# Linear attention in front of a gated layer: chunks of 128 steps worked as two halves, with a new order written out in the source

## The chip, the core and the metric

The kernel runs on one core of a Trainium2 chip. Its time is the device time of one execution in microseconds (us). The kernel before takes 587.41 us (median of 3 runs, 586.96 to 587.76). A change is called no change where it lies within 0.2%, about 1.2 us.

The core has a matrix engine (TensorE, PE in the profile; its weight loads are listed apart as PEld), VectorE (DVE), ScalarE (ACT) and GpSimd (POOL). Each runs its own list of instructions in order and waits for the others by semaphores. SyncE (SP) issues nearly all transfers.

## The reference

Four batches, 8 heads, 768 steps, 48 numbers a head. A state of 48x48 per batch and head decays by `w` at each step and takes in `k v`; the outputs of all heads, 384 numbers a token, go through a gated layer of width 1536.

```python
for t in range(S):
    cur = np.einsum('bhd,bhe->bhde', u[None] * kt, vt)
    y[:, :, t] = np.einsum('bhd,bhde->bhe', rt, state + cur)
    state = wt[:, :, :, None] * state + np.einsum('bhd,bhe->bhde', kt, vt)
...
g = x @ w_gate;  silu = g * (1.0 / (1.0 + np.exp(-g)));  val = x @ w_val
return silu * val @ w_out
```

## The kernel before

**Attention.** The 768 steps of a batch are cut into 6 chunks of 128 steps, 24 chunks in all (`n`, one batch after the other). Two heads share the 112 partitions of a tile (rows 0 to 47 and 64 to 111), so there are four pairs `p`, each with heads `j` = 0 and 1. For a chunk, `scan` and `scan2` (VectorE) make running products of `w`, `kq` and `re` scale `k` and `r` by them. On TensorE, `kb` transposes the scaled `k` (tile `kb`, copied out by `kn` on ScalarE), `sc` multiplies `k` and `r` into 128x128 scores per head, `dl` makes the chunk's addition to the state, and `y` sums the output from the scores (`at`, with `vt` and `vz`) and from the state before the chunk (`kr` with `sp`). `diag` puts the `u` term on the diagonal of `at` with eight ScalarE products of 128x128; `pred` (VectorE, twice, one for each `j`) copies the scores above the diagonal over it. `sps`, `spb` and `st` carry the state (VectorE, ScalarE, VectorE). `xh` and `xl` split the output into two parts; for the first ten chunks `xm` on TensorE makes the difference for `xl`. In `sc`, `dl` and `y` the operands are fp32, and the trace shows each such product as two passes (two MATMUL records).

**Gated layer.** The tokens form groups of 4, 2, 4, 4, 4, 4, 2 chunks. For each of 12 slices `f` of the width, `gv` runs 9 products for the gate (j=0) and 9 for the value (j=1) over all tokens of the group, `silu`, `sg`, `hh`, `hl` turn them into two parts, and `po` adds them to the group's output with 3 products a chunk. `ob` and `out` store it.

**Weights.** They arrive as 64-bit words (`raw`) and are turned into two parts by `top`, `low`, `upper` (ScalarE) and `shift`, `sign`, `plus`, `lower` (VectorE), for each `f` once. The first group's `gv` of slice `f` waits for it.

**Order.** A table `ORDER` holds the first part of the work, to the end of group 2; each name in it issues one step on its engine. From group 3 on a loop (`attention_steps` and `behind`) spreads the attention, three pieces to a chunk, between blocks of the gated layer. `spin` issues idle products at the start, which keep TensorE's clock up while it has nothing to do. In PSUM the attention has a pool `psA` with two buffers of one bank, `gv` two banks and `po` four.

Of the kernel before, what the change touches and what calls it, by code (L numbers as in the profile page):

```python
# [39 lines left out]
FREE = 3  # L40
# [3 lines left out]
TAKEN = 10  # L44

AGAIN = 10
# [1 line left out]
spin:21 uh ws:0 kr:0 ws:1 kr:1 raw:0 vt:0 scan:0 vt:1 kr:2 ub:0 seed:0 whole:0 raw:1 prod:0 kq:0
kr:3 scan2:0 kb:0 spin:6 re:0 kn:0 ws:2 diag:0:0 prod:1 sc:0 spin:19 scan:1 diag:0:1 pred:0:0
whole:1 seed:1 kq:1 top:0 pred:0:1 scan2:1 dl:0 spin:7 low:0 st:0 ws:3 shift:0 kb:1 vz:1 vz:0 re:1  # L50
y:0 sign:0 kn:1 diag:1:0 sc:1 spin:11 vt:2 prod:2 kr:4 diag:1:1 plus:0 xh:0 pred:1:0 raw:2 upper:0
xm:0 spin:9 pred:1:1 xl:0 sps:1 lower:0 top:1 dl:1 spin:10 spb:1 st:1 shift:1 low:1 y:1 spin:5
scan:2 sign:1 whole:2 xh:1 vt:3 vz:2 kr:5 xm:1 spin:7 sps:2 xl:1 kq:2 spb:2 plus:1 kb:2 spin:5
seed:2 kn:2 raw:3 prod:3 upper:1 dl:2 spin:13 scan2:2 diag:2:1 st:2 ws:4 re:2 diag:2:0 lower:1
sc:2 spin:18 top:2 scan:3 low:2 pred:2:0 kq:3 vz:3 seed:3 whole:3 kb:3 pred:2:1 scan2:3 y:2 spin:4
kn:3 diag:3:0 shift:2 ws:5 re:3 vt:4 xh:2 sps:3 sc:3 diag:3:1 sign:2 xm:2 spin:8 spb:3 pred:3:0
xl:2 pred:3:1 top:3 dl:3 plus:2 y:3 spin:12 low:3 st:3 raw:4 scan:4 upper:2 vt:5 prod:4 xh:3
lower:2 vz:4 xm:3 spin:5 whole:4 xl:3 gv:0:0:0 kq:4 shift:3 seed:4 sign:3 gv:0:0:1 silu:0:0
scan2:4 top:4 plus:3 vz:5 ws:6 gv:0:1:0 low:4 re:4 raw:5 upper:3 sg:0:0 kb:4 scan:5 hh:0:0
gv:0:1:1 kn:4 lower:3 whole:5 diag:4:0 hl:0:0 diag:4:1 sc:4 seed:5 shift:4 po:0:0 sps:4 silu:0:1  # L60
sign:4 spb:4 top:5 sg:0:1 gv:0:2:0 plus:4 hh:0:1 low:5 hl:0:1 raw:6 pred:4:1 gv:0:2:1 upper:4
pred:4:0 silu:0:2 lower:4 po:0:1 sg:0:2 shift:5 hh:0:2 prod:5 dl:4 sign:5 gv:0:3:0 top:6 kq:5
low:6 st:4 gv:0:3:1 plus:5 hl:0:2 upper:5 raw:7 sps:5 kb:5 scan2:5 silu:0:3 po:0:2 nat:6 kn:5
diag:5:0 sg:0:3 ws:7 lower:5 hh:0:3 gv:0:4:0 hl:0:3 shift:6 re:5 po:0:3 silu:0:4 sign:6 top:7
scan:6 low:7 y:4 plus:6 whole:6 gv:0:4:1 diag:5:1 vt:6 seed:6 ru:6 raw:8 ruk:6 upper:6 a0:6 kr:6
gv:0:5:0 sg:0:4 nat:7 diag:6:0 lower:6 vz:6 hh:0:4 gv:0:5:1 shift:7 xh:4 spb:5 hl:0:4 sign:7
silu:0:5 po:0:4 top:8 sg:0:5 plus:7 hh:0:5 xm:4 gv:0:6:0 low:8 kq:6 raw:9 hl:0:5 upper:7 scan2:6
gv:0:6:1 silu:0:6 lower:7 ws:8 xl:4 re:6 sc:5 shift:8 po:0:5 sg:0:6 sign:8 hh:0:6 top:9 hl:0:6
gv:0:7:0 low:9 plus:8 scan:7 upper:8 raw:10 gv:0:7:1 pred:5:0 silu:0:7 whole:7 seed:7 lower:8
po:0:6 sg:0:7 shift:9 hh:0:7 gv:0:8:0 pred:5:1 sign:9 top:10 y:5 hl:0:7 low:10 plus:9 po:0:7  # L70
silu:0:8 kr:7 ru:7 upper:9 raw:11 ruk:7 a0:7 diag:6:1 lower:9 vt:7 kb:6 nat:8 gv:0:8:1 kn:6
shift:10 xh:5 diag:7:0 kq:7 xm:5 gv:0:9:0 sign:10 xl:5 sg:0:8 plus:10 hh:0:8 sc:6 top:11 gv:0:9:1
hl:0:8 pred:6:0 upper:10 pred:6:1 scan2:7 po:0:8 silu:0:9 low:11 lower:10 ws:9 vz:7 dl:6 ru:8 y:6
shift:11 gv:0:10:0 sg:0:9 diag:7:1 kr:8 vt:8 sign:11 hh:0:9 st:6 gv:0:10:1 plus:11 hl:0:9 upper:11
kb:7 re:7 po:0:9 silu:0:10 ruk:8 vz:8 lower:11 kn:7 a0:8 gv:0:11:0 sg:0:10 diag:8:0 nat:9 scan:8
hh:0:10 gv:0:11:1 sps:7 whole:8 kq:8 spb:7 seed:8 hl:0:10 scan2:8 silu:0:11 po:0:10 xh:6 ru:9
ws:10 re:8 ruk:9 xm:6 gv:1:0:0 sg:0:11 xl:6 a0:9 hh:0:11 gv:1:0:1 scan:9 nat:10 sc:7 hl:0:11
whole:9 seed:9 silu:1:0 po:0:11 pred:7:1 sg:1:0 pred:7:0 hh:1:0 ru:10 dl:7 ob:0:0 hl:1:0 gv:1:1:0
ob:0:1 ruk:10 out:0:0 out:0:1 st:7 y:7 sps:8 silu:1:1 po:1:0 diag:8:1 vt:9 kr:9 kb:8 gv:1:1:1
diag:9:0 a0:10 nat:11 gv:1:2:0 spb:8 sg:1:1 hh:1:1 gv:1:2:1 xh:7 hl:1:1 vz:9 silu:1:2 kn:8 po:1:1  # L80
sg:1:2 ob:0:2 kq:9 hh:1:2 out:0:2 xm:7 ob:0:3 gv:1:3:0 scan2:9 xl:7 out:0:3 sc:8 hl:1:2 ws:11 re:9
# [36 lines left out]
def recurrence_then_glu_kernel(  # L118
# [114 lines left out]

    def shift(f):
        ints[f] = wst.tile([P, 3, DM], U32, tag="s", name=f"s_{f}", bufs=1)
        t = raws[f][:, :, :, 1].bitcast(U32)
        keep(nc.vector.tensor_scalar(ints[f], t, 0x1FFFFFFF, 3, ALU.bitwise_and, ALU.logical_shift_left))

    def sign(f):
        t = raws[f][:, :, :, 1].bitcast(U32)  # L240
        keep(nc.vector.scalar_tensor_tensor(ints[f], t, 0x80000000, ints[f], ALU.bitwise_and, ALU.bitwise_or))
# [536 lines left out]
```

## Time and profile before

| | |
|---|---|
| median of 3 runs | 587.41 us |
| profiled execution, first to last instruction | 585.2 us |
| TensorE busy | 570.4 us, 97% |
| VectorE, ScalarE busy | 325.1 us, 283.9 us |
| first `gv` starts | 46.59 us |
| last `po` ends | about 577.7 us |

Busy time of TensorE counts idle products too, and a matmul's record includes the time that it takes to run through the array, so that records overlap. For what a step costs, the start of the next one is read, not the length of a record. A group row reads: line, engine, operation, written tile <- read tiles, rows*columns of the weights, moving operand, count | busy us, mean ns of one | idle time before it and what ended it. A timeline row begins with the start and the length in us.

### The profile page before, as it was taken

Reading aid. Unit: us, or ns where it says so; the run is one execution under the profiler, and the core shown is the slowest. Engines: PE = TensorE matmul, PEld = TensorE weight load, DVE = VectorE, ACT = ScalarE, POOL = GpSimd, SP = SyncE. Lnnn points to the kernel's source line nnn. Section 1 sums busy time; section 2 is a strip of 40 time slices with the busy share of each in tenths; the row PEclk is TensorE's granted clock in tenths of the full one; section 3 lists DMA queues with packets and bytes.
Section 4 is the critical chain, followed back from the end, with each engine's and each line's share of the span. In section 5 each row is a group of like instructions: output and inputs, shape, how many; then the busy total and the mean of one; then the engine's idle time right before and its main releaser. Section 6 shows DMA issues by size and latency. Waiting matters only on the chain.

```text
span 585.2 us, 12525 instructions
## 1 busy us (share of the span) xinstructions
PE 570.4 (97%) x5333; PEld 494.4 (84%) x5333; DVE 325.1 (56%) x511; ACT 283.9 (49%) x639; POOL 1.8 (0%) x11
## 2 busy tenths in 40 slices
PE   7999999999999999999999999999999999999994
PEld 5777888889999888788888888888888888889994
DVE  6999999995655349751456365446344332222221
ACT  5798766864546236551525334475556422122221
POOL 1000000000000000000000000000000000000000
...
GB/s 302 262 129 192 125 222 168 176 89 123 92 61 62 55 48 138 115 55 1 106 39 89 41 50 88 103 88 96 62 74 62 55 2 0 1 1 7 48 1 33
DMA packets 22334, 50.63 MB, mean 87 GB/s; under 512 B 2592, under 2 KB 8864, under 8 KB 22272
## 3 DMA queue, kind: packets, MB, share of 16 engines
...
q8 instruction: 44, 0.72, 0.5%
...
q10 hardware_dynamic: 16, 0.00, 0.0%
...
## 4 chain that ended last, share of the span: by engine, by line
PE 83%; ACT 6%; DMA 5%; DVE 4%; issue 1%; SPq 0%; ACTq 0%; DVEq 0%
PE gv L541 46%; PE po L575 24%; PE y L441 5%; PE sc L385 4%; DMA raw<-in_wo_dram 2%; PE idle L608 2%; ACT at L346 1%; PE kb L361 1%; PE dl L409 1%; ACT raw L227 1%; DVE et L306 1%; DMA kr<-in_kr_dram 1%; DMA u_two<-in_u_rows_dram 1%; ACT raw L232 1%; ACT w_h L248 1%
## 5 line engine op out<-in xcount | busy, mean ns | idle before, releaser
L541 PE MATMUL gv<-xh,w_h 128*128 128x512 f32 (+1 forms) x504 | 183.7, 365 | 0.0
L541 PE MATMUL gv<-xl,w_h 128*128 128x512 f32 (+1 forms) x504 | 182.0, 361 | 0.0
L541 PE MATMUL gv<-xh,w_l 128*128 128x512 f32 (+1 forms) x504 | 181.6, 360 | 0.0
L553 DVE TENSOR_TENSOR sg<-sg,gv 128x512 f32<-128x512 f32 (+1 forms) x84 | 51.1, 608 | 141.4 <-PE gv L541 138.3
L541 PEld LDWEIGHTS gv<-xh,w_h 128*128 128x128 f32 x504 | 94.7, 188 | 15.1 <-issue 1.8
L541 PEld LDWEIGHTS gv<-xl,w_h 128*128 128x128 f32 x504 | 94.7, 188 | 15.0
L541 PEld LDWEIGHTS gv<-xh,w_l 128*128 128x128 f32 x504 | 94.8, 188 | 12.9
L575 PE MATMUL po<-w_h,hh 128*128 128x384 f32 x288 | 100.8, 350 | 0.5 <-ACT hh L558 0.5
L575 PE MATMUL po<-w_h,hl 128*128 128x384 f32 x288 | 97.2, 337 | 0.3 <-DVE hl L563 0.3
L558 ACT ACTIVATE hh<-sg 128x512 fp32r<-128x512 f32 (+1 forms) x84 | 47.8, 569 | 101.2 <-DVE sg L553 89.4
L575 PE MATMUL po<-w_l,hh 128*128 128x384 f32 x288 | 96.8, 336 | 0.0
L550 ACT ACTIVATE sg<-gv 128x512 f32<-128x512 f32 (+1 forms) x84 | 44.6, 531 | 90.8 <-PE gv L541 81.5
L563 DVE TENSOR_TENSOR hl<-sg,hh 128x512 fp32r<-128x512 f32 (+1 forms) x84 | 51.5, 613 | 51.1 <-ACT hh L558 50.7
L575 PEld LDWEIGHTS po<-w_h,hh 128*128 128x128 f32 x288 | 54.0, 188 | 7.5 <-issue 4.6
L575 PEld LDWEIGHTS po<-w_h,hl 128*128 128x128 f32 x288 | 54.1, 188 | 2.2 <-DVE hl L563 1.1
L575 PEld LDWEIGHTS po<-w_l,hh 128*128 128x128 f32 x288 | 54.0, 188 | 0.0
L346 ACT ACTIVATE at<-ident,a 128x128 f32<-128x128 f32 x144 | 45.6, 390 | 5.6 <-PE y L441 4.2
L390 DVE COPY_PREDICATED at<-mask,sc 128x512 f32<-128x512 uint32 x48 | 33.3, 730 | 8.7 <-PE sc L385 8.6
L317 ACT ACTIVATE ws<-ws 112x517 f32<-112x517 f32 x24 | 15.3, 638 | 35.3 <-DVE et L306 22.0
L289 DVE TENSOR_TENSOR_SCAN qt<-ws,d1q 112x516 f32<-112x516 f32 x24 | 29.4, 1226 | 1.8 <-DMA ws<-in_wt_dram 1.7
L306 DVE TENSOR_TENSOR_SCAN et<-ws,d1e 112x516 f32<-112x516 f32 x24 | 29.4, 1225 | 1.5 <-ACT pend L294 1.4
L385 PE MATMUL sc<-kr 48*64 48x128 f32 x768 | 28.6, 282 | 1.3 <-ACT kn L371 0.5
...
## 6 DMA issues: line engine op xcount, KB each, us to landing
...
```

The costliest lines, as they stand in the source:

```text
L289: keep(nc.vector.tensor_tensor_scan(_flat(qts[n])[:, ::-1], wss[n][:, 1:][:, ::-1], _flat(d1q)[:, ::-1], 0.0, ALU.mult, ALU.add))
L306: keep(nc.vector.tensor_tensor_scan(_flat(ets[n]), wss[n][:, :L], _flat(d1e), 0.0, ALU.mult, ALU.add))
L346: keep(nc.scalar.activation(a[:, p, :], ident, AF.Copy, scale=d))
L385: pin(nc.tensor.matmul(scs[n][j][ms, p, :], krs[n][o, 0, p, ms], krs[n][o, 1, p, :], start=True, stop=True,))
L390: keep(nc.vector.copy_predicated(ats[n, j], mask4, scs[n][j]))
L441: pin(nc.tensor.matmul(ys[n][32 * q : 32 * q + 32, b // 4, :], lhs, rhs, start=start[q] == i, stop=stop[q] == i,))
L541: pin(nc.tensor.matmul(ps, a[:, f, j, q * P : (q + 1) * P], x[:, q, :], start=m == 0, stop=m == 3 * NK - 1,))
L550: keep(nc.scalar.activation(sgs[g, f], ps, AF.Silu))
L553: keep(nc.vector.tensor_tensor(sgs[g, f], sgs[g, f], gvs.pop((g, f, 1)), ALU.mult))
L558: keep(nc.scalar.activation(hhs[g, f], t, AF.Copy))
L563: keep(nc.vector.tensor_tensor(hls[g, f], t, hhs[g, f].bitcast(F32), ALU.subtract))
L575: pin(nc.tensor.matmul(pos[g][j], a[:, ts], x[:, f, 2, :], start=f == 0 and i == 0, stop=f == NF - 1 and i == 2,))
```

## The change

1. **Halves.** Each chunk is worked as two halves of 64 steps (`HC`). `sc` makes only the two 64x64 blocks on the diagonal of the scores. What the second half takes from the first goes through the state: `dl` makes both halves' additions apart, `mid` adds the first to the state, and `y` reads the state twice (`spa` for the first half, `spb` for the second). The score part of `y` is made of products with 64 rows and 64 columns instead of 128 and 128. Scores and additions of a chunk share one tile of two banks (`s`), a half or a head to each bank; the output has a tile of two banks under the same tag, and `psA` has one buffer, so `s` and `y` of all later chunks take turns in it. `kb` of the next chunk uses the free part of the output's tile from chunk 6 on.
2. **Diagonals.** `diag` is one VectorE product of 128x512 with a broadcast operand, and `pred` one instruction instead of two.
3. **Signs.** `sign` masks 16-bit half words in place instead of a two-operand step over 32-bit words, and `shift` does one operation.
4. **Chunks across batches.** Chunk n is now chunk n // 4 of batch n % 4. Only chunks 0 to 3 start without a state, and only 20 to 23 end a batch.
5. **Order.** The table holds all of the work; the loop is gone. The first `gv` runs in two halves (`a`, `b`) of the group's tokens, `po` also chunk by chunk (`c0` to `c3`). `xm` is used for four chunks instead of ten. There are 126 idle products instead of 160.
6. One tile `d1` serves both scans; `zero` (GpSimd) clears its first column between them. Odd stores of the last group go over ScalarE's queue.

The core of the diff:

```diff
+HC = C // 2
-TAKEN = 10
+TAKEN = 4
-spin:21 uh ws:0 kr:0 ws:1 kr:1 raw:0 vt:0 scan:0 vt:1 kr:2 ub:0 seed:0 whole:0 raw:1 prod:0 kq:0
...
+uh ws:0 kr:0 scan:0 whole:0 seed:0 prod:0 vt:1 kq:0 kr:1 spin:40 kb:0 scan2:0 ws:1 kn:0 vt:0 re:0
...
-    psA = ctx.enter_context(tc.tile_pool(name="psA", bufs=2, space=PSUM))
+    psA = ctx.enter_context(tc.tile_pool(name="psA", bufs=1, space=PSUM))
...
+    def sign(f):
+        t = raws[f].bitcast(U16)
+        keep(nc.vector.tensor_scalar(t[:, :, :, 1], t[:, :, :, 3], 0x8000, None, ALU.bitwise_and))
-        keep(nc.vector.scalar_tensor_tensor(ints[f], t, 0x80000000, ints[f], ALU.bitwise_and, ALU.bitwise_or))
...
+    place = [n % B * NCH + n // B for n in range(NC)]
...
+    def zero(n):
+        keep(nc.gpsimd.memset(d1[:, :, 0:1], 0.0))
...
-                keep(nc.scalar.activation(a[:, p, :], ident, AF.Copy, scale=d))
+            keep(nc.vector.tensor_tensor(
+                ats[n], ident2.unsqueeze(1).unsqueeze(1).to_broadcast(shape),
+                d.rearrange("s p j -> s j p").unsqueeze(3).to_broadcast(shape), ALU.mult,
+            ))
...
+    def s_of(n):
+            pool, tag, bufs = (psM, "po", 2) if n < GROUPS[0] else (psA, "pa", 1)
+            ss[n] = pool.tile([P, 2, BANK], F32, tag=tag, name=f"s_{n}", bufs=bufs)
+    def y_of(n):
+            ys[n] = psA.tile([P, 2, BANK], F32, tag="pa", name=f"y_{n}")
...
     def sc(n):
-                        scs[n][j][ms, p, :], krs[n][o, 0, p, ms], krs[n][o, 1, p, :], start=True, stop=True,
+                        s[ms, j, p, :], krs[n][o, 0, p, ms], krs[n][o, 1, p, ms], start=True, stop=True,
...
+    def dl(n):
+        first, second = slice(0, HC), slice(HC, C)
+        parts = [[(0, first)], [(1, slice(0, C))]] if n < B else [[(0, first), (1, second)]]
+        for part_ in parts if n // B < NCH - 1 else [[(0, first)]]:
+            for p in range(NPR):
+                for lo, hi, j in ((0, 32, 0), (32, 64, 0), (64, 96, 1), (96, PR, 1)):
+                    for r, o in part_:
...
+    def mid(n):
+        keep(nc.vector.tensor_tensor(t, dl_of(n, 0), t, ALU.add))
+    def spb(n):
+        blocks(n, 1, dl_of(n, 0) if n < B else state[n % B])
...
     def y(n):
+        for h in range(0 if n >= B else 1, 2):
+            o = slice(HC * h, HC * h + HC)
+                    todo.append((3 * p + i, h, sps_[h][:, p, 32 * i : 32 * i + 32], r[:, p, o]))
...
+                    pairs_[g, j // 2] = psM.tile([P, 2, BANK], F32, tag="po", name=f"po_{g}_{j // 2}", bufs=2)
...
+            if g == len(GROUPS) - 1 and j % 2:
+                queue = nc.scalar
```

Three places show how the order moves. The first is TensorE's own start. In the kernel before its list begins with idle products, the transposed `u` and the first `kb`; the last of 21 idle products and what follows read:

```order
L608 LDWEIGHTS mask
L608 MATMUL idle<-mask 128x256
L323 MATMUL u_turned<-ident,u_two 112x8
L361 MATMUL kb_171<-ident,kr_141 128x112
L363 MATMUL kb_171<-u_head,prod_165 128x2
```

In the changed kernel it begins like this, and the idle products at its head are 40:

```order
L395 MATMUL u_turned<-ident,u_two 112x8
L687 LDWEIGHTS ident
L687 MATMUL idle<-ident 128x256
...
L462 MATMUL kb_182<-ident,kr_129 128x112
L464 MATMUL kb_182<-u_head,prod_135 128x2
```

`u_turned`, which waits for the small transfer `u_two`, now stands ahead of all idle products, and 40 of them stand between it and the first `kb`.

The second place is VectorE's first stretch, from the second scan of chunk 0 on (`kr` is written by `kq` and then by `re`, `at` by `diag` and `pred`). Before:

```order
L306 SCALAR_TENSOR_TENSOR et_169<-ws_139,d1e 112x516
L312 TENSOR_TENSOR kr_141<-kr_141,et_169 112x512
L328 TENSOR_TENSOR prod_196<-kr_145 112x512
L289 SCALAR_TENSOR_TENSOR qt_235<-ws_143,d1q 112x516
L390 COPY_PREDICATED at_0_191<-mask,sc_0_198 128x512
L297 RECIPROCAL d1e<-qt_235 112x4
L301 TENSOR_TENSOR kr_145<-kr_145,qt_235 112x512
L390 COPY_PREDICATED at_1_237<-mask,sc_1_199 128x512
```

Now:

```order
L375 SCALAR_TENSOR_TENSOR et_191<-ws_127,d_89 112x516
L384 TENSOR_TENSOR kr_129<-kr_129,et_191 112x512
L358 SCALAR_TENSOR_TENSOR qt_260<-ws_193,d_89 112x516
L400 TENSOR_TENSOR prod_265<-kr_140 112x512
L422 TENSOR_TENSOR at_267<-ident_81,kn_195 128x512
L366 RECIPROCAL d_89<-qt_260 112x4
L488 COPY_PREDICATED at_267<-mask_86,s_209 128x512
L370 TENSOR_TENSOR kr_140<-kr_140,qt_260 112x512
```

The diagonal product (L422) is new on VectorE and reads `kn`, which comes from the first `kb`; the second predicated copy is gone.

The third place is TensorE at a chunk in the middle. In the kernel before, chunk 13 has `sc` alone between blocks of the gated layer, and later `dl` and `y` together:

```order
L541 MATMUL gv_6_1_2984<-xl_1679,w_h 128x512
L385 MATMUL sc_0_3005<-kr_2838 64x128 x2
L385 MATMUL sc_1_3006<-kr_2838 64x128 x2
...
L409 MATMUL dl_3057<-vt_2846,kn_2997 32x48 x3
L409 MATMUL dl_3057<-vt_2846,kn_2997 16x48
...
L441 MATMUL y_3074<-kr_2838,sp 32x128 x12
L441 MATMUL y_3074<-at_0_2840,vt_2846 32x128
L441 MATMUL y_3074<-at_0_2840,vz_93 32x128
```

Now, at chunk 12, `dl` stands directly ahead of `sc` in one tile, gated-layer products follow, and `y` stands alone:

```order
L501 MATMUL s_3409<-vt_3071,kn_3330 32x48 x6
L501 MATMUL s_3409<-vt_3071,kn_3330 16x48 x2
...
L482 MATMUL s_3409<-kr_3069 64x64 x16
L651 MATMUL po_0_2893<-w_h,hh_6_3326 128x384
...
L559 MATMUL y_3508<-kr_3069,sp_92 32x64 x12
L559 MATMUL y_3508<-kr_3069,sp_93 32x64 x12
L559 MATMUL y_3508<-at_3251,vt_3071 32x64
L559 MATMUL y_3508<-at_3251,vz_96 32x64
```

`dl` has moved ahead of the gated-layer blocks that separate `sc` from `y`; it has twice the products, `sc` half the columns, and `y` twice the products with half the columns.

More of the change, by code (lines that the diff above doesn't have):

```diff
@@ L37 @@
 PEND_MIN = 1e-15
[L40 removed]
+BANK = 512
 SUMMED = 6
[L44 to L46 removed]
+TAKEN = 4
+ON_ACT = ()
+SHARED = 6
 ORDER = """
[L48 to L51 removed]
@@ L52 @@
[L52 to L81, printed above, removed]
@@ new lines @@
+raw:0 spin:5 sc:0 dl:0 vz:0 zero:0 scan:1 spb:0 whole:1 prod:1 diag:0 seed:1 pred:0 kq:1 spin:16 y:0
+top:0 scan2:1 kb:1 kr:3 kr:2 ws:2 re:1 prod:2 zero:1 low:0 xh:0 kn:1 raw:1 st:0 shift:0 sign:0
+scan:2 kq:2 kr:4 spin:6 dl:1 vt:2 xm:0 st:1 seed:2 spin:20 kb:2 diag:1 xl:0 plus:0 vz:2 kn:2 whole:2
+scan2:2 sc:1 ws:3 upper:0 zero:2 re:2 pred:1 vz:1 low:1 raw:2 spb:1 prod:3 scan:3 kq:3 spin:18 sc:2
+spin:7 y:1 vt:3 top:1 diag:2 sign:1 dl:2 xh:1 kb:3 top:2 whole:3 spb:2 pred:2 seed:3 xm:1 lower:0
@@ new lines @@
+scan2:3 shift:1 xl:1 spin:14 gv:0:0:1:a low:2 plus:1 kn:3 y:2 xh:2 re:3 dl:3 gv:0:0:0:a spb:3 vz:3
+silu:0:0:a st:2 xm:2 sc:3 diag:3 sg:0:0:a zero:3 hh:0:0:a xl:2 pred:3 vt:4 upper:1 hl:0:0:a y:3 xh:3
+po:0:0:c1 xm:3 xl:3 vz:4 ws:5 st:3 raw:3 ws:4 po:0:0:c0 sign:2 gv:0:0:0:b lower:1 silu:0:0:b shift:2
+plus:2 scan:4 gv:0:0:1:b upper:2 raw:4 sg:0:0:b top:3 hh:0:0:b gv:0:1:1 gv:0:1:0 lower:2 low:3
+prod:4 hl:0:0:b shift:3 sign:3 silu:0:1 po:0:0:c3 sg:0:1 kr:5 po:0:0:c2 hh:0:1 low:4 plus:3 whole:4
@@ new lines @@
+upper:3 hl:0:1 gv:0:2:1 sign:4 raw:5 gv:0:2:0 silu:0:2 po:0:1 top:4 kq:4 vt:6 lower:3 sg:0:2 shift:4
+hh:0:2 seed:4 plus:4 kb:4 gv:0:3:0 kn:4 low:5 upper:4 gv:0:3:1 scan2:4 raw:6 hl:0:2 sign:5 silu:0:3
+top:5 lower:4 sps:4 sg:0:3 shift:5 po:0:2 plus:5 re:4 prod:5 hh:0:3 gv:0:4:1 hl:0:3 gv:0:4:0 dl:4
+sc:4 spa:4 top:6 zero:4 upper:5 lower:5 shift:6 silu:0:4 low:6 sign:6 sg:0:4 ws:6 raw:7 po:0:3
+gv:0:5:1 plus:6 hh:0:4 scan:5 hl:0:4 diag:4 gv:0:5:0 low:7 upper:6 silu:0:5 po:0:4 top:7 seed:5
+lower:6 sg:0:5 hh:0:5 mid:4 spb:4 gv:0:6:0 sign:7 hl:0:5 shift:7 plus:7 whole:5 raw:8 ub low:8
@@ new lines @@
+pred:4 gv:0:6:1 st:4 silu:0:6 upper:7 top:8 sg:0:6 lower:7 po:0:5 raw:9 y:4 gv:0:7:0 sign:8 shift:8
+plus:8 xh:4 hh:0:6 low:9 upper:8 hl:0:6 silu:0:7 kq:5 gv:0:7:1 top:9 scan2:5 lower:8 sg:0:7 po:0:6
+hh:0:7 shift:9 sign:9 raw:10 kb:5 kn:5 gv:0:8:1 plus:9 raw:11 hl:0:7 xl:4 gv:0:8:0 sps:5 low:10
+upper:9 top:10 lower:9 zero:5 po:0:7 vt:5 kr:6 ws:7 nat:6 silu:0:8 shift:10 sign:10 sg:0:8 gv:0:9:0
+hh:0:8 plus:10 low:11 hl:0:8 upper:10 silu:0:9 top:11 re:5 diag:5 lower:10 spa:5 gv:0:9:1 po:0:8
+dl:5 sg:0:9 sc:5 shift:11 sign:11 mid:5 hh:0:9 vz:5 gv:0:10:1 spb:5 plus:11 gv:0:10:0 hl:0:9 po:0:9
@@ new lines, in po @@
+    def po(g, f, h=""):
+        if h[:1] == "c":
+            tiles = [int(h[1:])]
+            h = next(k for k in ("", "a", "b") if (g, f, k) in hhs and tiles[0] in range(*part(g, k)))
+        else:
+            tiles = range(*part(g, h))
+        t0 = part(g, h)[0]
+        high, low_ = hhs[g, f, h], hls[g, f, h]
+        for j in tiles:
+            if f == 0:
+                if (g, j // 2) not in pairs_:
+                    pairs_[g, j // 2] = psM.tile([P, 2, BANK], F32, tag="po", name=f"po_{g}_{j // 2}", bufs=2)
+                pos[g, j] = pairs_[g, j // 2][:, j % 2, :DM]
+            ts = slice((j - t0) * P, (j - t0 + 1) * P)
+            for i, (a, x) in enumerate(((high, w_h), (low_, w_h), (high, w_l))):
```

487 lines of the change are left out of this document (247 added, 240 removed).

## The prediction, made before the changed kernel ran

> **What bounds the kernel now.** I read the page's busy times first, then the slices, then the chain that ended last.
>
> ```profile
> span 585.2 us, 12525 instructions
> PE 570.4 (97%) x5333; PEld 494.4 (84%) x5333; DVE 325.1 (56%) x511; ACT 283.9 (49%) x639; POOL 1.8 (0%) x11
> PE   7999999999999999999999999999999999999994
> DVE  6999999995655349751456365446344332222221
> PE 83%; ACT 6%; DMA 5%; DVE 4%; issue 1%; SPq 0%; ACTq 0%; DVEq 0%
> ```
>
> TensorE is busy from the second slice to the last but one; VectorE is as full only in the first nine slices. Part of that TensorE time is idle products, so I cut the span at the first `gv` (46.59), at the first `gv` of group 1 (133.47) and at the last `po`, and ask for the idle products (L608) alone.
>
> ```profile
> 0.00:46.59 46.59, 41.19 (x669) 32.52 (x670) 40.96 (x60) 35.27 (x76) 1.84 (x11) 0.96 0.73 235
> 46.59:133.47 86.88, 86.35 (x687) 73.84 (x684) 83.25 (x108) 59.72 (x108) 0.00 (x0) 1.00 0.48 157
> 133.47:578.00 444.53, 442.82 (x3982) 388.06 (x3981) 200.61 (x345) 188.94 (x456) 0.00 (x0) 1.00 0.20 58
> 578.00:585.20 7.20, 0.00 (x0) 0.00 (x0) 0.29 (x1) 0.00 (x0) 0.00 (x0) 0.64 0.19 65
> 0.00:46.59 46.59, 22.60 (x160) 15.85 (x160) 0.96 0.73 235
> ```
>
> Columns after the length: PE, PEld, DVE, ACT, POOL busy, granted clock, DMA. Before the first `gv` TensorE does 41.19 - 22.60 = 18.6 us of work and loses 28.0 us, while VectorE is busy for 41 of 46.6 us: it sets the start. From 46.59 to 578 TensorE idles 0.5 + 1.7 us in all. The end costs 7.2 us. So the span is about 585.2 - 28.0 - 2.2 - 7.2 = 547.8 us of TensorE work plus 37.4 us lost, and the change is worth what it takes from either.
>
> **Prices on TensorE.** One `sc` between gated-layer products, and one `dl` with `y`:
>
> ```profile
> 209.00 0.34 PE L575 MATMUL po<-w_l,hh 128*128 128x384 f32 x1
> 209.27 1.10 PE L385 MATMUL sc<-kr 48*64 48x128 f32 x32
> 210.30 0.44 PE L575 MATMUL po<-w_h,hh 128*128 128x384 f32 x1
> ...
> 212.58 0.54 PE L409 MATMUL dl<-vt,kn 128*32 128x48 f32 x32
> 212.95 0.83 PE L441 MATMUL y<-kr,sp 112*32 112x128 f32 x24
> 213.60 0.28 PE L441 MATMUL y<-at,vt 128*32 128x128 f32 x1
> ...
> 214.59 0.50 PE L541 MATMUL gv<-xh,w_h 128*128 128x512 f32 x1
> 214.93 0.40 PE L541 MATMUL gv<-xh,w_l 128*128 128x512 f32 x1
> 215.16 0.39 PE L541 MATMUL gv<-xl,w_h 128*128 128x512 f32 x1
> ```
>
> From start to next start, `sc` takes 1.03 us for 32 passes of 128 columns; the 24 state passes of `y` 0.65 us (27.1 ns each, 128 columns); the 32 score passes 0.99 us; the 32 passes of `dl` 0.37 us (11.6 ns each, 48 columns). The last two prices give 15.5 ns for 80 columns, so a pass of 64 columns should take 11.6 + 16 x 0.194 = 14.7 ns. Going from one shape to another costs about 0.1 us: the first `gv` product behind `y` takes 0.34 us to the next start, the second 0.23.
>
> Row halves: the passes of `sc` have 64-column weights, so only two fit beside each other; 27.1 x 32 = 0.87 us of its 1.03 can only be met if the two row halves (heads) run at once. For pieces of 64 rows by 32 columns, which `dl` and the score part of `y` become, there is no row. Two halves at once would make it 7.3 ns a pass at 64 columns, one after the other 14.7. Starts in the rows above lie 11.6 ns apart in the mean. I take 8 ns, nearer to `sc`, the only row with two halves, and keep 7.3 and 14.7 as ends.
>
> **The change, part by part.**
>
> - *`sc`*: 32 passes of 64 columns, 32 x 14.7 ns + the 0.16 us that 1.03 has over 0.87 = 0.63 us: -0.40 x 24 = -9.6 us. Ends: everything halves, -0.52 x 24 = -12.4; or as it stands, 0.
> - *`y`*: 48 state passes (24 chunks less the first four have both halves) 0.71 us, 64 score passes at 8 ns 0.51, a shape change between 0.10: 1.32 against 1.64, -0.32 x 20 = -6.4 us. For chunks 0 to 3, 24 + 64 passes, 0.96 against 0.99 without state: nothing. Ends for all 24: 64 passes at 7.3 without the change of shape, -9.9; at 14.7, +4 us.
> - *`dl`*: 64 passes instead of 32. At 8 ns 0.51 against 0.37: +0.14 x 20; chunks 20 to 23, which had none, 32 passes +0.3 x 4: +4.0 us. Ends: +0.8; at 11.6 ns +8.9.
> - *`kb`*: the four last chunks of a batch had none: four transposes there. *`xm`*: six fewer.
>
> ```profile
> 222.14 0.55 PE L361 MATMUL kb<-ident,kr 112*128 112x112 f32 x4
> 222.61 0.86 PE L441 MATMUL y<-kr,sp 112*32 112x128 f32 x24
> L454 PE MATMUL y<-xh,minus 128*128 128x384 f32 x10 | 3.8, 377 | 1.5 <-ACT xh L450 1.5
> ```
>
>   `kb` takes 0.47 us to the next start: +1.3 to +1.9, I take +1.3, as most stand beside other attention work. An `xm` is one `po`-sized product (0.17 us between starts) and two shape changes: -0.37 x 6 = -2.2.
> - *`dl` beside `sc`*: a change of shape more in each chunk, 0.1 x 24 = +2.4; end 0.
> - *VectorE and ScalarE*: `diag` moves from ScalarE to VectorE and `pred` halves.
>
> ```profile
> L346 ACT ACTIVATE at<-ident,a 128x128 f32<-128x128 f32 x144 | 45.6, 390 | 5.6 <-PE y L441 4.2 <-DVE a L338 1.1
> L390 DVE COPY_PREDICATED at<-mask,sc 128x512 f32<-128x512 uint32 x48 | 33.3, 730 | 8.7 <-PE sc L385 8.6
> L301 DVE TENSOR_TENSOR kr<-kr,qt 112x512 f32<-112x512 f32 x24 | 16.5, 688 | 17.7 <-DMA kr<-in_kr_dram 17.6
> L241 DVE SCALAR_TENSOR_TENSOR s<-raw,s 128x1152 uint32<-128x1152 uint32 x12 | 16.2, 1350 | 0.0
> L237 DVE TENSOR_SCALAR s<-raw 128x1152 uint32<-128x1152 uint32 x12 | 9.1, 757 | 0.1
> L289 DVE TENSOR_TENSOR_SCAN qt<-ws,d1q 112x516 f32<-112x516 f32 x24 | 29.4, 1226 | 1.8 <-DMA ws<-in_wt_dram 1.7
> L245 DVE CUSTOM_DVE_ANT_0 s<-raw,s 128x2304 uint16<-128x2304 uint16 x12 | 16.6, 1383 | 0.0
> L251 DVE TENSOR_TENSOR w_l<-s,w_h 128x1152 fp32r<-128x1152 f32 x12 | 16.2, 1348 | 1.2 <-ACT w_h L248 1.2
> L418 DVE TENSOR_TENSOR st<-dl,st 112x192 f32<-112x192 f32 x16 | 5.6, 348 | 2.1 <-PE dl L409 2.1
> L403 ACT ACTIVATE sp<-st 48x192 f32<-48x192 f32 x40 | 14.4, 359 | 3.9 <-DVE st L395 2.9
> ```
>
>   VectorE: +24 x 0.69 for `diag` (a two-operand product of 512, as L301), -24 x 0.73 for `pred`, -12 x 0.59 for `sign` if it costs what `shift` does, +20 x 0.35 for `mid`: about zero. ScalarE loses some 60 us and gains 48 copies, 17 us. After 133.47 VectorE is busy for 201 of 444 us, so these cost nothing there; if that cover went, half a microsecond of wait per chunk would be 10 us in all. `zero` is a 0.1 to 0.4 us job on an idle GpSimd between two scans.
>
> **The start.**
>
> ```profile
> 2.54 4.42 PE L608 MATMUL idle<-mask 128*128 128x256 bf16 x21 [2.54 <-POOL mask L176]
> 7.55 0.19 PE L323 MATMUL u_turned<-ident,u_two 8*112 8x8 f32 x1 [0.59 <-DMA u_two<-in_u_rows_dram]
> 7.67 0.32 PE L361 MATMUL kb<-ident,kr 112*128 112x112 f32 x1
> 46.59 0.48 PE L541 MATMUL gv<-xh,w_h 128*128 128x512 f32 x1
> ...
> 65.76 0.54 PE L409 MATMUL dl<-vt,kn 128*32 128x48 f32 x32
> ```
>
> `u_turned` waits for its transfer until 7.5 us, and now all idle products stand behind it. 40 of them take 4.42 us for the first 21 and 19 x 0.131 (the other 139 of the 22.60 us) = 6.9 us: the first `kb` starts near 14.6 us, not 7.67. VectorE's list meets `diag` of chunk 0 after 6.6 us of work and waits there for `kn`, till about 16.4: some 10 us behind its own sum. Added up with the prices above, VectorE has 28.8 us of work up to the first half `gv` (43.4 us up to the first `gv` before), so that one starts near 38.5 us. But chunks 2 and 3 come after it. Walking on by these prices, slice 1's `po` ends near 60.6 us; in the kernel before `dl` of chunk 4 follows that `po` at 65.76, with `kb` and `sc` of that chunk done as well (2.2 us). Lost time until then: 7.6 us at the head, 126 idle products 19.2, together 26.8 against 28.0. I book -1 us, with ends -6 (`kb` comes earlier than that) and +6 (VectorE delays the first slices).
>
> **Waits later, and the end.** `s` and `y` of later chunks share one buffer: `y` waits for `mid`, `spb`, `st` (0.35 + 0.72 + 0.35 us), the next `sc` for `xh`, `xl`, `kn` (about 1.6 us). Between them the new order puts 3 to 13 us of gated-layer products in most places, and none between `xl` and `sc` in three chunks. I book +2, ends 0 and +20. Two queues for the last stores: -0.3.
>
> Sum: -9.6 - 6.4 + 4.0 + 1.3 - 2.2 + 2.4 - 1 + 2 - 0.3 = -9.8 us on 585.2, a span of 575.4. The median of the runs lies 2.2 us above the profiled span: **577.5 us**.
>
> **Rivals.**
>
> *Dense* (chance 0.17): halves run fully at once, shape changes hide, the start gains. -12.4 - 9.9 + 0.8 + 1.3 - 2.2 - 4 = -26: 561 us. For it: `sc`'s 27 ns. Against it: no row has eight pieces at work.
>
> *A floor of 11.6 ns a pass* (0.10): `dl` has fewer columns than any other and shows no shorter pitch than 11.6; if that is the pace at which passes can start, `y`'s 64 cost 0.74 and `dl`'s 64 too. -9.6 - 1.8 + 8.9 + 1.3 - 2.2 + 2.4 + 1 = 0: 587.5, no change. The Trainium skill, "TensorEngine Tiling (Array Packing)", section "Instruction Overhead", goes further: about 60 cycles per matmul on TRN2 however few its columns, so that a dimension already small should not be split; and "TensorE: Matmul & The Clock Gate", section "Wait — 56ns, not 53.3ns?", puts the least time between two starts at about 25 ns. By that figure the 208 passes of `sc`, `dl` and `y` would take an estimated 5.2 us a chunk, and the kernel would get some 40 us slower; the trace does not agree for pieces beside each other, with 11.6 ns a pass in `dl`, so this form gets 0.02. On the other side its section "Tiling Modes" lists 64x32 as eight tiles, which would put `dl` and the scores at the dense end; no run here shows that yet.
>
> *The shared buffer decides* (0.11, the slower one): at each of 20 chunks TensorE waits for the chain `dl`, `mid`, `spb`, `y` or `y`, `xl`, `sc`. At 1 us a chunk +20 - 11.8: about 596; it turns slower from 0.5 us a chunk on. For it: one buffer instead of two, and VectorE's queue holds `sg` and `hl` ahead of `mid`. Against it: the cover above, and only 2.2 us of idling before.
>
> *The start is lost* (0.05): the late `kb` costs all that the halves give there, +6: about 584.
>
> *The halved columns bring nothing* (0.02): weight loads set the pitch, `y` gets 112 passes at 27 ns: over 610. 11.6 ns in `dl` speaks against it.
>
> **Numbers.** The forecast has the rest, 0.53, with a range of its own of 570 to 584. Faster by over 0.2% (which is what a measurement here can tell): 0.53 + 0.17 + 0.05 + 0.03 of the floor = 0.78; same 0.05, the middle of the floor; slower 0.17. The range of 562 to 593 leaves out the better half of *dense* and most of the slower cases.
>
> **What would show it.** `sc` near 0.6 us from start to next start; `dl` and the score part near 0.5 us each, by which the halves are settled; the first `kb` near 14.6 us and the first `gv` near 38.5; TensorE idle from there to the last `po` at 2 to 6 us. Wrong it is if `sc` keeps 1 us, if the rows of `y` or `sc` show idle time before them of half a microsecond or more each, or if VectorE's waits for `kn` hold the start beyond 46 us.

## The result, and the profile after

The changed kernel takes 597.22 us (median of 4 runs, 594.68 to 598.55) where the kernel before took 587.59 beside it (4 runs, 586.96 to 588.40): ratio 1.0160, interval 1.0135 to 1.0185. It is 1.6% slower; the forecast was 577.5, with a range to 593. The profiled execution took 594.68 us, 593.0 of them from first to last instruction, 7.8 more than before.

The page of the changed kernel, the lines that answer to those shown of the kernel before, and the queue of TensorE's instructions:

```profile
span 593.0 us, 16649 instructions
PE 569.4 (96%) x7443; PEld 496.4 (84%) x7443; DVE 331.2 (56%) x541; ACT 256.7 (43%) x493; POOL 5.1 (1%) x35
PE   4888899999999999999999999999999999999995
DVE  4687889988777555745556446355435333432222
PEclk9799999999999999999999999999999999999999
q8 instruction: 60, 0.98, 0.7%
PE 84%; ACT 6%; DVE 4%; issue 2%; DMA 2%; SPq 0%; DVEq 0%; ACTq 0%
```

TensorE is less than full in its first five slices now, not only in the first. The span cut at the first `gv`, at the first `gv` of group 1 and near the end of the last `po`, then the idle products alone (columns as in the prediction; the last two are the transfers' share and GB/s):

```profile
0.00:46.05 46.05, 33.91 (x643) 27.34 (x643) 30.01 (x47) 21.57 (x32) 3.09 (x16) 0.89 0.55 166
46.05:142.60 96.55, 91.24 (x1083) 76.75 (x1084) 83.27 (x104) 68.61 (x79) 0.21 (x2) 0.98 0.44 148
142.60:586.70 444.10, 444.10 (x5719) 392.35 (x5718) 217.37 (x391) 166.01 (x381) 1.80 (x17) 1.00 0.22 65
586.70:593.00 6.30, 0.11 (x1) 0.00 (x0) 0.56 (x1) 0.49 (x1) 0.00 (x0) 0.90 0.23 75
0.00:46.05 46.05, 19.08 (x126) 13.70 (x126) 0.89 0.55 166
```

The loss lies in one stretch, group 0. The first `gv` comes at 46.05 (before 46.59), but group 0 then takes 96.55 us instead of 86.88, with TensorE idle for 5.3 us of them and at a clock of 0.98. From 142.60 on TensorE is busy without a break, for 444.10 us (before 444.53), and in that time it also does the attention of chunk 6, which the kernel before had behind it at 133.47. The end takes 6.3 instead of 7.2 us.

Three things stand out in the first two stretches. The first is a group on ScalarE and one on VectorE; the third line is the kernel before:

```profile
L295 ACT ACTIVATE raw<-raw 128x1152 uint16<-128x1152 uint32 x12 | 33.8, 2820 | 2.4 <-DMA raw<-in_wo_dram 2.4
L302 DVE TENSOR_SCALAR raw<-raw 128x1152 uint16<-128x1152 uint16 x12 | 17.8, 1485 | 5.2 <-ACT raw L295 3.4 <-ACT pend L363 1.6 <-ACT raw L291 0.2
L232 ACT ACTIVATE raw<-raw 128x1152 int32<-128x1152 uint32 x12 | 15.5, 1290 | 0.0
```

`low` writes 16-bit half words now and takes 2820 ns instead of 1290, 18.3 us more in all; `sign` waits for it and takes 1485 ns, where I had 757. The list of what was changed names only `sign` and `shift`; that `low` was narrowed as well is not in it.

The second is VectorE at the head, and the third a gap in the middle of `y` of chunk 0 (timelines of VectorE and TensorE, start and length first; the bracket is idle time before it and its releaser):

```profile
15.14 0.69 DVE L400 TENSOR_TENSOR prod<-kr 112x512 f32<-112x512 f32 x1 [3.79 <-PE kb L464]
...
18.01 0.74 DVE L488 COPY_PREDICATED at<-mask,s 128x512 f32<-128x512 uint32 x1 [1.49 <-ACT sp L515]
...
25.14 0.69 DVE L400 TENSOR_TENSOR prod<-kr 112x512 f32<-112x512 f32 x1 [3.75 <-PE kb L464]
...
41.60 0.73 DVE L488 COPY_PREDICATED at<-mask,s 128x512 f32<-128x512 uint32 x1 [1.69 <-ACT sp L515]
...
19.71 0.22 PE L559 MATMUL y<-at,vt 64*32 64x64 f32 x1
22.01 0.26 PE L559 MATMUL y<-at,vz 64*32 64x64 f32 x1 [2.08 <-issue]
```

The first `kb` starts at 13.85 us, behind 40 idle products, and VectorE waits for it, at `prod` of chunk 1 and not first at `diag`, as the prediction had it. Its second wait of that size comes for the larger part from the gap: TensorE stands still for 2 us between two products of one step, with nothing in the profile to wait for ("issue"), and `kb` of chunk 1 comes late. The clock follows (stretches of 5 us):

```profile
15.00:20.00 5.00, 4.92 (x169) 3.86 (x170) 3.27 (x6) 3.39 (x7) 0.00 (x0) 1.00 0.89 288
20.00:25.00 5.00, 2.99 (x50) 2.82 (x50) 1.35 (x2) 2.56 (x2) 0.10 (x1) 0.67 0.56 163
25.00:30.00 5.00, 5.00 (x87) 3.92 (x88) 4.83 (x7) 1.24 (x3) 0.00 (x0) 0.65 0.07 21
```

In the steady part, a chunk's products on TensorE:

```profile
207.27 0.79 PE L501 MATMUL s<-vt,kn 64*32 64x48 f32 x64
207.99 0.69 PE L482 MATMUL s<-kr 48*64 48x64 f32 x32
208.62 0.45 PE L651 MATMUL po<-w_h,hh 128*128 128x384 f32 x1
...
218.65 0.88 PE L559 MATMUL y<-kr,sp 112*32 112x64 f32 x48
219.46 0.24 PE L559 MATMUL y<-at,vt 64*32 64x64 f32 x1
220.25 0.60 PE L462 MATMUL y<-ident,kr 112*128 112x112 f32 x4
```

From start to next start `dl` takes 0.72 us, `sc` 0.63, the state passes of `y` 0.81 and its scores 0.79.

### The profile page after: what moved, and what is told of

It reads as the page before. It is cut to its first block, busy times and chain, and to the rows that moved or that the text cites. A ratio compares the mean times of both kernels' runs of the same rounds, so it can differ in the third digit from the quotient of the medians.

```text
span 593.0 us, 16649 instructions
## 1 busy us (share of the span) xinstructions
PE 569.4 (96%) x7443; PEld 496.4 (84%) x7443; DVE 331.2 (56%) x541; ACT 256.7 (43%) x493; POOL 5.1 (1%) x35
## 4 chain that ended last, share of the span: by engine, by line
PE 84%; ACT 6%; DVE 4%; issue 2%; DMA 2%; SPq 0%; DVEq 0%; ACTq 0%
PE gv L610 45%; PE po L651 23%; PE y L559 6%; ACT raw L295 4%; PE s L501 3%; PE idle L687 2%; PE s L482 2%; DMA raw<-in_wo_dram 2%; PE y L462 1%; DVE raw L302 1%; DVE w_l L317 1%; ACT w_h L314 1%; DMA ws<-in_wt_dram 1%; DVE sg L623 1%; PE kb L462 1%
## 5 line engine op out<-in xcount | busy, mean ns | idle before, releaser
L610 PE MATMUL gv<-x,w_h 128*128 128x512 f32 (+1 forms) x996 | 292.7, 365 | 1.7 <-DVE sg L623 0.9
L610 PEld LDWEIGHTS gv<-x,w_h 128*128 128x128 f32 x996 | 179.8, 189 | 31.5 <-DVE sg L623 1.5
L610 PE MATMUL gv<-x,w_l 128*128 128x512 f32 (+1 forms) x498 | 179.8, 361 | 0.8 <-DVE w_l L317 0.8
L610 PEld LDWEIGHTS gv<-x,w_l 128*128 128x128 f32 x498 | 94.0, 189 | 13.5 <-DVE w_l L317 1.5
L515 ACT ACTIVATE sp<-st 48x192 f32<-48x192 f32 x80 | 28.7, 359 | 16.2 <-DVE st L522 13.0
L295 ACT ACTIVATE raw<-raw 128x1152 uint16<-128x1152 uint32 x12 | 33.8, 2820 | 2.4 <-DMA raw<-in_wo_dram 2.4
L358 DVE TENSOR_TENSOR_SCAN qt<-ws,d 112x516 f32<-112x516 f32 x24 | 29.4, 1226 | 4.1 <-DMA ws<-in_wt_dram 3.9
L375 DVE TENSOR_TENSOR_SCAN et<-ws,d 112x516 f32<-112x516 f32 x24 | 29.5, 1228 | 2.0 <-ACT pend L363 1.1
L488 DVE COPY_PREDICATED at<-mask,s 128x512 f32<-128x512 uint32 x24 | 17.7, 737 | 9.9 <-PE s L501 3.9
L559 PE MATMUL y<-at,vz 64*32 64x64 f32 x768 | 20.9, 225 | 2.1 <-issue 2.1
```

Of the source, the lines that this page charges most:

```text
L295: keep(nc.scalar.activation(raws[f].bitcast(U16)[:, :, :, 0], raws[f][:, :, :, 0].bitcast(U32), AF.Copy, scale=2.0**-29,))
L358: keep(nc.vector.tensor_tensor_scan(_flat(qts[n])[:, ::-1], wss[n][:, 1:][:, ::-1], _flat(d1)[:, ::-1], 0.0, ALU.mult, ALU.add))
L375: keep(nc.vector.tensor_tensor_scan(_flat(ets[n]), wss[n][:, :L], _flat(d1), 0.0, ALU.mult, ALU.add))
L515: keep(nc.scalar.activation(sps_[i][o, :, j * D : (j + 1) * D], t[o], AF.Copy))
L559: pin(nc.tensor.matmul(y_of(n)[32 * q : 32 * q + 32, h, b // 4 * HC : b // 4 * HC + HC], lhs, rhs, start=start[q, h] == i, stop=stop[q, h] ...
L610: pin(nc.tensor.matmul(ps, a[:, f, j, q * P : (q + 1) * P], x[:, q, lo * P : hi * P], start=m == 0, stop=m == 3 * NK - 1,))
```

## The experiments

Times are set against the kernel before on the same chip; between comparisons only the ratios are put side by side. 0.1% is 0.6 us. Lines of `ORDER` are shortened in the diffs, and a trace is of one execution only. Points 4 and 6 of the change, and the order behind its head, were not undone by themselves.

**Both half words undone** in the changed kernel:

```diff
-        keep(nc.scalar.activation(
-            raws[f].bitcast(U16)[:, :, :, 0], raws[f][:, :, :, 0].bitcast(U32), AF.Copy, scale=2.0**-29,
+        t = raws[f][:, :, :, 0]
+        keep(nc.scalar.activation(t, t.bitcast(U32), AF.Copy, scale=2.0**-29))
...
-        keep(nc.vector.tensor_scalar(t[:, :, :, 1], t[:, :, :, 3], 0x8000, None, ALU.bitwise_and))
+        keep(nc.vector.scalar_tensor_tensor(ints[f], t, 0x80000000, ints[f], ALU.bitwise_and, ALU.bitwise_or))
...
```

> The changed kernel with the half words undone: low writes 32-bit words again and sign is the old or of two operands, put behind shift; all else is kept. Theory W (the half words are what the start of group 0 lost): ScalarE's low goes from 2820 to about 1290 ns, 18.3 us less ScalarE in the first 142 us, VectorE's sign from 1485 to 1350 ns; the first product of group 1 starts 5 us or more earlier than 142.6, and the time is 590 to 592 us. Theory H (the head sets it: 40 idle products and the first kb at 13.85 us, then a TensorE that waits for nothing in y of chunk 0): the first gv stays within 1 us of 46.05 and the time within 1.5 us of 597.2.

588.53 us, ratio 1.0036 (1.0011 to 1.0062); group 1 starts at 135.09 instead of 142.60. A little better than theory W, and far from H, though the first `gv` moves by 1.6 us only.

**The head alone:**

```diff
-uh ws:0 kr:0 scan:0 whole:0 seed:0 prod:0 vt:1 kq:0 kr:1 spin:40 kb:0 ...
+spin:21 uh ws:0 kr:0 scan:0 whole:0 seed:0 prod:0 vt:1 kq:0 kr:1 spin:12 kb:0 ...
```

> The changed kernel with the head of the order changed alone: 21 idle products ahead of u_turned as before the change, then 12 in place of 40, so the first kb can start near 9.2 us and not at 13.85. Theory H: VectorE's wait of 3.8 us for that kb goes, what follows moves up by 3 to 4 us, and the time is 593 to 594.5. Theory W: the weight chain (low on ScalarE) decides when the first slices have their weights; the first gv starts at most 1.5 us earlier, the time is 596 to 597.5.

591.20 us, ratio 1.0098 (1.0062 to 1.0134), 3.6 us less than the changed kernel by the ratios: H holds as well. The first `kb` starts at 7.64, the first `gv` at 39.93, group 1 at 137.06.

**Both edits:**

> Both edits, 32-bit words and the earlier head. If the two losses lie one behind the other, the gains add up: about 587 to 589. If one hides behind the other, the time is that of the better one alone, 590 to 594. If a third thing holds the start (TensorE's work itself, which the steady part has at nearly no gain), it stays above 595.

585.59 us, ratio 0.9975 (0.9943 to 1.0007). The two gains of 1.2% and 0.6% add up; this kernel can't be told from the one before.

**The half words alone, in the kernel before** (the first diff the other way round):

> The kernel before with the half words alone (low to 16 bits, sign as a 16-bit and, shift with one operation). Theory W: low costs 2820 ns there too, ScalarE gets 18.3 us more in the first 133 us and VectorE 1.6 us, the chain raw, top, low, sign, plus, upper, lower gets 1.5 us longer a block, and the time goes up by 2 to 6 us, 590 to 593. Rival: ScalarE has the room (60 of 87 us busy between 46.6 and 133.5 us) and only VectorE's 1.6 us shows: 588 to 589.

591.78 us, ratio 1.0096 (1.0058 to 1.0134): theory W, 5 us for steps that I had costed as a small saving. `low` takes 2833 ns there, so its price does not come from the new order.

**The gap in `y`.** In these traces the gap stands at the same count of TensorE's records (weight loads and products in order of their starts), though the earlier head put other products there. That suggested blocks of instructions, and two kernels that only put more products ahead of `u_turned`:

```diff
-spin:21 uh ws:0 ...
+spin:6 tiny:87 uh ws:0 ...
+    def tiny(times):
+        for _ in range(times):
+            pin(nc.tensor.matmul(idle[:32, :32], busy[:32, :32], busy[:32, :32], start=True, stop=True))
```

> The third kernel here (32-bit words, earlier head) with 72 more products at the head, 6 idle and 87 tiny ones (32 rows by 32 columns) in place of 21 idle, while TensorE waits for u_two anyway; nothing else moves. They stand for 144 instructions. Theory F (TensorE's instructions come in blocks of 256 over queue 8, two of them held; where a block runs out before the next has landed, TensorE stands still: the trace has the gaps in y of chunk 0 and dl of chunk 2 at the same record, 443 or 444 and 1208 or 1209, in all four kernels, whatever the head): the block ends move by 144 records against the work, the gap of 3.6 us in y of chunk 0 and the one of 1.6 in dl of chunk 2 go (under 1 us each), one of about 1.5 us appears near record 1720, in dl of chunk 3; the time is 1 to 4 us below the third kernel's. Rival C (the gap belongs to the place: cold clock, loads, a wait that the trace does not show): it stays in y of chunk 0 at over 2 us, and the time stays within 1 us.

> The same with 36 more products at the head, 12 idle and 45 tiny ones: 72 instructions. Theory F: the first gap stays in y of chunk 0 but 36 passes earlier in it (again near record 444), and a second one comes in dl of chunk 1 or 2, at a block end again (near record 700 or 1212); time as the third kernel's or up to 1.5 us less. Rival C: gaps at the same passes as in the third kernel.

584.24 us, ratio 0.9943 (0.9921 to 0.9964), and 583.68 us, ratio 0.9933 (0.9913 to 0.9953); the second gains more than was said. Counted from the traces, the gaps of this kind (record, us from start to next start):

```
changed kernel            443: 2.3               1208: 1.5
32-bit words              443: 2.7               1208: 1.5
earlier head              444: 3.4               1209: 1.5
both                      444: 3.9               1209: 1.8
72 more products                     698: 2.0                1974: 2.3
36 more products          444: 1.0   698: 3.7
92 more products                     699: 1.1
```

All stand at 443 or 444 or a multiple of 255 records behind it, whatever product is there: in `y` of chunk 0 or in `dl` of chunk 2 before, in `dl` of chunk 1 with 36 more. In each of them TensorE starts again 1.3 to 1.7 us after a packet of queue 8, which brings instructions, has landed (changed kernel: landed at 20.4 and 39.1, next start at 22.0 and 40.5). Rival C is out. The places were foretold for the kernel with 36 more, not for the one with 72: its gap at 698 was not, and the other came at 1974, while near 1720 there are 0.6 us. TensorE's timeline of the kernel with 36 more, `dl` of chunk 1:

```profile
17.94 0.83 PE L509 MATMUL s<-vt,kn 64*32 64x48 f32 x44 [0.32 <-ACT kn L479]
22.26 0.69 PE L509 MATMUL s<-vt,kn 128*32 128x48 f32 x20 [3.48 <-issue]
```

The Trainium skill, "Runtime: NRT & Kernel Launch", section "Instruction fetch mechanics", says that an engine's instructions arrive in blocks of 16 KiB, 256 each, over a queue of its own; the 60 packets of 0.98 MB in all on queue 8 and the 255 records agree. It also says that TensorE holds 2048 and that the fetch is hidden because instructions issue slowly. That does not agree with these gaps.

**More products still**, to put the block ends elsewhere (`spin:6 tiny:107`):

> The same kernel with 92 more products at the head than the third one had, 6 idle and 107 tiny. Theory F (blocks of 256 instructions): the block ends lie 184 records earlier against the work, at the dl of chunk 0, then in kb of chunk 1, in sc of chunk 1 and in y of chunk 1; the shortest stretch of 256 instructions before 30 us is then 3.9 us and not 3.0, so the gaps before 30 us sum to at most 2.5 us instead of 4.6, in kb of chunk 1 if anywhere; time 581.5 to 583.5. Rival: what the kernel with 36 more products gained is the warm clock alone, and the place of the gaps doesn't matter: 583 to 585.

582.71 us, ratio 0.9937 (0.9918 to 0.9956). The gaps before 30 us fell to 1.7 us in sum, as said (0.8 of it before a `kb` at record 894, which is no block end), but the time is that of the kernel with 36 more. No gain from shorter gaps there is seen.

**Later loads**, with the 36 products and without:

```diff
-... kb:1 kr:3 kr:2 ws:2 re:1 prod:2 zero:1 low:0 xh:0 kn:1 raw:1 st:0 ...
+... kb:1 kr:2 ws:2 re:1 prod:2 zero:1 low:0 xh:0 kn:1 st:0 ...
-... dl:1 vt:2 xm:0 ...
+... dl:1 vt:2 kr:3 raw:1 xm:0 ...
```

> The kernel with 36 more products at the head, with the loads raw of block 1 and kr of chunk 3 issued behind vt of chunk 2, some 5 us later; both are first used after 30 us. Theory L (a block of instructions is late because its transfer stands among 1.6 MB of loads that aren't needed yet: the transfers are busy to 1.0 from 5 to 20 us and the fetch starts 3 to 6 us after the block before it ran out, against 1 us where they are quiet): the fetches near 12 and 19.6 us start 1 to 3 us earlier, the gaps of 1.0 and 3.5 us in y of chunk 0 and dl of chunk 1 shrink to under 2 us together, prod of chunk 1's wait for kr goes as well, and the time is 580 to 582. Rival (the sequencer itself is late): gaps as before, time 583 to 584.5.

> The same two loads issued later in the third kernel, without the products at the head. Theory L: the gap of 3.6 us in y of chunk 0 shrinks to under 2 us and stays at record 444; time 1 to 4 us below the third kernel's. Rival: the gap keeps its 3.6 us.

581.91 us, ratio 0.9924 (0.9891 to 0.9956), and 583.76 us, ratio 0.9954 (0.9932 to 0.9976). In the first the second fetch (packet on queue 8) starts at 15.0 instead of 19.6 us and the gap of 3.7 us goes; in the other the gap at record 444 shrinks from 3.9 to 2.3, not to under 2. So loads that stand ahead are a part of why a block is late (theory L). In time, 0.1 and 0.2% are within the intervals: a gain is not shown. And the next fetch, behind the moved loads, is 6 us late in its turn.

**`diag` back on ScalarE** for all chunks, with the 36 products:

```diff
-ON_ACT = ()
+ON_ACT = tuple(range(24))
```

> The kernel with 36 more products at the head (32-bit words, earlier head), with diag on ScalarE again for all chunks, eight copies each of 64 columns; this is the part of the change that moved diag, undone. The prediction costed that move at nothing. If so: time within 1.5 us of 583.7. If VectorE's 16 us had been what the start could not bear: faster by 2 us or more. If ScalarE's eight copies (about 8 x 0.3 us between kn and pred, on the way of y) are on the path: slower by 2 to 6 us, most of it before 140 us.

586.85 us, ratio 1.0001 (0.9978 to 1.0024) against 0.9933. Moving `diag` to VectorE is worth some 4 us. Its copies, 192 in all:

```profile
L427 ACT ACTIVATE at<-ident,a 128x64 f32<-128x64 f32 x144 | 36.2, 335 | 5.2 <-DVE a L418 5.1
L427 ACT ACTIVATE at<-ident,kn 128x64 f32<-128x64 f32 x48 | 12.0, 338 | 0.0
```

They put 48 us on ScalarE; group 1 starts at 132.53 instead of 129.16.

**Orders inside `dl` and `y`:**

```diff
+        pairs = (2, 3, 0, 1) if n >= B and n % 4 == 2 else range(NPR)
...
+            if n >= B and n % 4 == 3:
+                steps = [(p, q, k) for k in part_ for p in pairs for q in quarters]
+            for _ in range(2 if n >= B and n % 4 == 1 else 1):
...
```

> The changed kernel with other orders inside dl and y of the chunks from 4 on, one look for the starts inside. Chunks n with n % 4 = 1: dl issued twice (128 passes, the same values), 2: head pairs in the order 2, 3, 0, 1 and the scores of y by time halves, 3: all of the first row half ahead of the second, scores reversed, 0: as it is. dl now runs its passes in eights at 66, 43, 42, 103, 132, 53, 80 ns and 97 with 0.1 for the change of shape, in every chunk alike. Theory Q (TensorE has some 24 passes waiting at the start of a burst and is then supplied with one each 11 ns or so): the slowness goes by position, so the second issue takes 64 x 11 = 0.70 us more, with no fast eights at its start, and the order of head pairs changes nothing. Theory P (some pieces collide, by place in the tiles or banks): the second issue repeats the same pattern, and another order of head pairs gives another one. All of one half first: 43 ns for four passes, 0.69 us in all; with both halves at once it would be 0.34.

A single run, 597.32 us. From start to next start `dl` takes 0.72 us with the pairs turned round, in the same eights; 0.78 with one half first; and issued twice 1.29:

```profile
126.33 1.36 PE L505 MATMUL s<-vt,kn 64*32 64x48 f32 x128
127.62 0.58 PE L482 MATMUL s<-kr 48*64 48x64 f32 x24
...
161.06 0.85 PE L505 MATMUL s<-vt,kn 64*32 64x48 f32 x64
161.84 0.69 PE L482 MATMUL s<-kr 48*64 48x64 f32 x32
```

The slowness goes by position, not by place: the second 64 passes show none of the eights of 42 to 43 ns that the first begin with (theirs take 53 ns and more) and cost 0.57 us, 8.9 ns a pass (theory Q, with 11 said). `y` by time halves takes 1.69 us instead of 1.60, with its scores reversed the same 1.60.

**`low` alone undone**, `sign` left as it is:

> The changed kernel with low alone undone: ScalarE writes whole 32-bit words again (0 to 7, the upper half zero), and sign stays the 16-bit and into that upper half. It parts the two half-word steps. If low's 1.53 us x 12 on ScalarE are all of what the first run gave back: ratio to the kernel before 1.002 to 1.006, low near 1290 ns, sign still near 1485. If sign (1485 ns, ready later than the old or, and the same bytes of raw written in turn by two engines) has a part in it: 1.008 to 1.014.

586.51 us, ratio 0.9974 (0.9946 to 1.0001).

```profile
L296 ACT ACTIVATE raw<-raw 128x1152 int32<-128x1152 uint32 x12 | 15.2, 1268 | 4.3 <-DMA raw<-in_wo_dram 4.3
L301 DVE TENSOR_SCALAR raw<-raw 128x1152 uint16<-128x1152 uint16 x12 | 17.8, 1481 | 0.0
```

Undoing `low` alone gives back 1.9% or 11 us, more than the whole loss and better than said, though the first `gv` starts at 46.70 here and group 1 at 135.46: what `low` costs, it costs in group 0. The 16-bit `sign`, which need not follow `shift`, is no loss but looks like a gain of some 0.6% over the 32-bit one of the first run, with head and gaps as they were; whether its type or its freer place makes that was not separated.

**All of it together** (late loads, head, 36 products, 32-bit `low`, 16-bit `sign`):

> The kernel with late loads (earlier head, 36 more products at the head, raw of block 1 and kr of chunk 3 later), with the 16-bit sign of the changed kernel and low in 32 bits. If the three losses are separate: low32 alone gave 0.9974 and the rest moved 1.0036 to 0.9924, so 0.984 to 0.988, 578 to 580 us, and what is then missing to the predicted 577.5 is small by accident, since TensorE's work lies above it. If they cover each other (the 16-bit sign gains only where VectorE waits for a late head): 0.990 to 0.993, 581 to 583 us.

581.03 us, ratio 0.9889 (0.9863 to 0.9914), between the two: part of the gains covers each other. It is the lowest ratio of all kernels here.

```profile
0.00:40.00 40.00, 35.30 (x665) 28.46 (x666) 28.73 (x46) 16.56 (x31) 2.51 (x15) 0.93 0.63 191
40.00:80.00 40.00, 39.03 (x548) 33.45 (x546) 35.66 (x44) 25.83 (x38) 0.68 (x2) 0.98 0.58 187
80.00:140.00 60.00, 59.91 (x701) 52.45 (x700) 55.70 (x76) 37.10 (x59) 0.21 (x2) 1.00 0.42 130
140.00:576.00 436.00, 435.23 (x5565) 383.36 (x5563) 209.81 (x378) 160.18 (x366) 1.68 (x16) 1.00 0.21 64
```

From 40 us on TensorE idles 1.8 us in all, so there is hardly a wait left there to take out.

## Why the prediction was wrong

It was 19.7 us too low, 17.6 by the profiled span (593.0 against 575.4). By its own steps:

- *VectorE and ScalarE*: the step that failed worst. "These cost nothing there" was said of the time after 133.47, and it held: from 142.60 on TensorE never waits. But group 0 lies before that, and for all that lies before the sum had only the -1 of the start, added up from prices among which `low` has none. `low` changed too; its price of 2820 ns is in none of the rows shown, and the weights of group 0 wait for it. Undone, it gives 11 us back. `sign` at `shift`'s price was wrong too (1485 ns, not 757), but no loss comes of it. `diag` on VectorE was costed at nothing and brings some 4 us, 3.4 of them before group 1.
- *The start, -1*: wrong in size and in mechanism. The first `kb` came at 13.85, close to the 14.6 said, but the first `gv` at 46.05 and not at 38.5, and the `po` of slice 1 ends near 70 and not near 60.6. VectorE's own work was about right (30.0 us busy until the first `gv`, 28.8 added up); what the walk had at nothing is the waits behind the first `kb`, 3.75, 1.49 and 1.69 us in the rows above. The late `kb`, which I had seen and let pass, costs 3.6 us (1.0160 to 1.0098). With the earlier head, the 36 products and 32-bit words the first `gv` does come at 38.58.
- *A cause that I did not have*: blocks of instructions. The halves turn 5333 products into 7443, the new ones 10 to 20 ns apart, and at the start such runs come close behind each other. The two kernels that move the block ends gain 0.3 and 0.4% over the one with both edits, with intervals that just overlap its own. The clock has a part in it: of the ten executions of the one with both edits, the five with a granted clock of 0.987 to 0.993 take 582.7 to 584.0 us, about what the one with 36 more takes at 0.990 to 0.996 (581.5 to 584.5, on a chip where the kernel before takes 0.2% longer), and the five at 0.982 to 0.984 take 587.2 to 588.5. How much of the gain is gap and how much clock was not separated.
- *`y`, -6.4*: 0.2 measured. The state passes take 0.81 us as said. The 64 score passes take 0.79, not 0.51: 10.2 ns a pass instead of 8, and the change of shape behind them (0.14), which I had left out. That is 1.60 against 1.64 for 20 chunks, and 0.47 + 0.79 against 0.99 for four.
- *`dl`, +4.0 and +2.4 for the shapes*: 9.0 measured, 0.36 x 20 and 0.47 x 4. Without the 0.1 for the shape a pass takes 9.6 ns, not 8.
- *`sc`, -9.6*: right, 0.625 us a chunk. *`kb`, +1.3*: right within 0.2. `xm` was not priced again.
- *Later waits, +2, and the shared buffer*: TensorE is busy for 444.10 of 444.10 us; the one buffer costs nothing there. That rival said 596 and was close by accident: its mechanism is absent. The end was 0.9 us shorter, not 0.3.

The terms on TensorE, with -2.2 kept for `xm`, come to -9.8 + 0.2 + 9.0 + 1.5 - 2.2 = -1.3 us instead of -10.5: 9.2 of the 17.6 us. The rest is what lies before group 1. The rival *a floor of 11.6 ns a pass* had this sum nearly right, for a wrong reason. There is no such floor: after the first eight of `dl`, 16 passes start 5.3 ns apart (eights of 42 to 43 ns) where one half alone, in chunks 20 to 23, needs 10.6 (eights of 85). The Trainium skill, "TensorEngine Tiling (Array Packing)", section "Tiling Modes", with its eight tiles of 64x32, agrees with the 5.3. The same page of the Trainium skill, section "Instruction Overhead", gives 60 cycles a matmul (the prediction worked with 25 ns); passes that start 8.9 to 10.2 ns apart do not agree with it. Its advice, not to split a dimension that is already small, is not tested by `dl`, which was split in its 128 rows and went from 0.37 to 0.72 us. Why a run falls from 5.3 to 8.9 ns a pass after some 24 passes is open; the doubled `dl` shows that it goes by position in the run.
